# Routing attention and a gated MLP on one core: two of the four score-mask products of a pair of heads are issued in other periods

## The chip, the cores and the metric

The kernel runs on one core of one Trainium2 chip. The metric is the device time of the program in microseconds (us), the median of several runs. Beside it there is one profiled execution, from which all durations of single instructions come. The engines are TensorE (PE; PEld is its weight load), VectorE (DVE), ScalarE (ACT), GpSimd (POOL) and SyncE (SP, which issues DMAs).

## The reference

Four batches of eight heads, 768 tokens, head dimension 64, 16 centroids for each head. Each query and each key goes to the centroid that it is most similar to; a query attends to the keys of the same centroid alone. A gated MLP follows, on 3072 tokens.

```python
def _attn_ref(q, k, v, centroids):
    ...
    q_assign = np.argmax(np.einsum('bhsd,hcd->bhsc', q_n, c_n), axis=-1)
    k_assign = np.argmax(np.einsum('bhsd,hcd->bhsc', k_n, c_n), axis=-1)
    mask = q_assign[:, :, :, None] == k_assign[:, :, None, :]
    scores = scale * np.matmul(q, k.transpose(0, 1, 3, 2))
    scores = np.where(mask, scores, -1000000000.0)
    scores = scores - np.max(scores, axis=-1, keepdims=True)
    attn = np.exp(scores)
    attn = attn / (np.sum(attn, axis=-1, keepdims=True) + 1e-09)
    return np.matmul(attn, v).astype(np.float32)

def _moe_ref(x, w_in, w_out):
    h = x @ w_in
    sp = np.maximum(h, 0.0) + np.log1p(np.exp(-np.abs(h)))
    return ((h * erf(sp)) @ w_out).astype(np.float32)
```

## The kernel before

**Pairs, halves, periods.** The 32 heads are worked on as 16 pairs (p = 0 to 15). A pair's two heads lie in partitions 0 to 63 (e = 0) and 64 to 127 (e = 1), so a matrix product over the 64 numbers of one head uses one half of the TensorE array's rows. Each pair has 12 units: two halves of 384 queries times six blocks of 128 keys. Two units make a period, so that a pair has six periods, i = 0 to 5 (`period(p, i)`, line 720). Periods 0 to 2 work on the first half of the queries, 3 to 5 on the second.

**Order.** Each engine takes its instructions in the order in which the program issues them (`InOrder`, line 55). So the order in which `period` calls things is the order on each engine. In a period TensorE gets:

1. in periods 0 and 3 `turn` (line 390): six small products that turn the row maxima into rows; ScalarE then writes them as two casts into the row "shift" of the mask tile `qm`;
2. `step_ahead(u)` (line 711), one step of the row maxima, mostly of the next pair: two products `wide<-kv,qv` and two `wide<-km,qm`, and after them a reduction on VectorE (`nmx<-wide`);
3. place 0 for a mask product;
4. `products` (line 410) of the two units: queries times keys, into two score banks `sc`, in fp32;
5. place 1 for a mask product;
6. `step_ahead(u + 1)`, as in 2;
7. `scores` (line 423) of the two units: four products `sc<-qm,km` in bf16 that add the mask and the shift to the score banks;
8. place 2 for a mask product;
9. in period 3 `similarities` of the pair after the next;
10. `attend` (line 453) of the two units of the period before: eight products `turned<-pr,in_v`, over all 128 rows;
11. in periods 0 and 3 the sums of the curves for the division (`turned<-more_out,minus`).

ScalarE gets, between these, `curve` of each of the two units (exp of the score bank, `pr<-sc`), and small jobs of the weights, which are brought into another number form during attention: in period 1 `size_and_rest`, in period 2 `sign` (line 245, tile `x_own` or `x_more`), in period 3 `size_and_rest`, in period 4 `sign` of a second piece, for as long as there are early pieces (22 of them, so `sign` of period 2 runs in pairs 1 to 11). Periods 4 and 5 also have a copy of the keys and of the queries into bf16 (`kv`, `qv`), and periods 0 and 3 the two casts of `turn`.

**Mask products.** The masks of the next pair come from `hotT`, which holds a one at each token's centroid: queries in partitions 0 to 63, keys in partitions 64 to 127. `masks(p, nm, half, bank)` (line 350) issues one bf16 product with `pick` as weights, over the 64 rows of queries or of keys, for one half of the tokens, and gives back the copy that is to follow on ScalarE: Relu into `qm` for queries, Identity with a bias tile and a scale into `km` for keys. Each pair needs four of them: ("q", 0), ("q", 1), ("k", 0), ("k", 1). The keys' two halves and the first half of the queries are read from period 3 on by `step_ahead`, the second half of the queries from period 0 of the next pair on.

`MASKS` (line 51) says in which period and place each is issued; pair 0 has a table of its own, `FIRST_MASKS`. A product goes into the bank `turned[0]` in periods 0 and 5 and into `turned[1]` in the others. These two banks also hold the value products (`turned[half]`) and the other small results, at other times. In places 0 and 1 the copy is issued at once after the product; in place 2 it is issued on ScalarE between the two curves:

```python
        mask(0)()
        ...
        mask(1)()
        if u > 0:
            step_ahead(u + 1)
        ...
        scores(u)
        scores(u + 1)
        later = mask(2)
        ...
        curve(u)
        later()
        curve(u + 1)
```

After attention the MLP runs from line 891 on, with products over all 128 rows.

Of the kernel before, what the change touches and what calls it, by code (L numbers as in the profile page):

```python
# [47 lines left out]
NPT = NJ + 2  # L48
N_LATE = 10
LAST_X = 11  # L50
MASKS = {(0, 1): ("k", 0), (0, 2): ("k", 1), (2, 0): ("q", 0), (5, 0): ("q", 1)}
FIRST_MASKS = {(2, 0): ("k", 0), (2, 1): ("q", 0), (2, 2): ("k", 1), (5, 0): ("q", 1)}


# [17 lines left out]
def kernel(  # L72
# [647 lines left out]
    def period(p, i):  # L720
# [4 lines left out]
        def mask(place):  # L725
            which = (MASKS if p else FIRST_MASKS).get((i, place))
            if which:
                return masks(p + 1, *which, turned[0 if i in (0, 5) else 1])
            return lambda: None
# [261 lines left out]
```

## Time and profile before

| | us |
|---|---|
| median of 3 runs | 1022.72 (1022.52 to 1022.75) |
| profiled execution | 1022.77 |
| its span, first to last instruction | 1021.1 |
| first and last value product of attention (`turned<-pr,in_v`), start | 24.7 and 435.9 |
| one pair (period 2 of pair 5 to period 2 of pair 6, first `sc`) | 26.39 (158.51 to 184.90) |
| a mask product, `turned<-hotT,pick`, 64 rows, 384 columns, median | 0.32 |
| copy of a key mask (`km<-turned,nbig`), mean | 0.58 |
| copy of a query mask (`qm<-turned`, 128 partitions), mean | 0.49 |
| one of the two casts of `turn` (`qm<-turned`, 1 partition), mean | 0.47 |
| a curve (`pr<-sc`), mean | 0.81 |
| mean granted clock of TensorE | 1.000 |

The profile's lines all name line 63, the helper that records each operation, so that instructions are told apart by their tiles: "out<-in". A matmul's duration is longer than what it holds the array for, since successive ones are pipelined; the start-to-start time tells what one costs. In the timeline, equal instructions that follow each other are merged into one line, with their number at its end. Tiles named `more_out` among the inputs of `sc` are transposed queries and keys of every third pair, which are kept there.

### The profile page before, as it was taken

Reading aid. Unit: us, or ns where it says so; the run is one execution under the profiler, and the core shown is the slowest. Engines: PE = TensorE matmul, PEld = TensorE weight load, DVE = VectorE, ACT = ScalarE, POOL = GpSimd, SP = SyncE. Lnnn points to the kernel's source line nnn. Section 1 sums busy time; section 2 is a strip of 40 time slices with the busy share of each in tenths; the row PEclk is TensorE's granted clock in tenths of the full one; section 3 lists DMA queues with packets and bytes.
Section 4 is the critical chain, followed back from the end, with each engine's and each line's share of the span. In section 5 each row is a group of like instructions: output and inputs, shape, how many; then the busy total and the mean of one; then the engine's idle time right before and its main releaser. Section 6 shows DMA issues by size and latency. Waiting matters only on the chain.

```text
span 1021.1 us, 15464 instructions
## 1 busy us (share of the span) xinstructions
PE 1013.9 (99%) x5930; PEld 726.1 (71%) x5930; DVE 695.8 (68%) x1305; ACT 515.0 (50%) x673; POOL 345.7 (34%) x229
## 2 busy tenths in 40 slices
PE   8999999999999999999999999999999999999998
PEld 3555555554555445478888888888888888888887
DVE  8777777777777777778875674756565547565754
ACT  3787877787777666567615142322233141505050
POOL 1777777777777667745130000000000000000000
PEclk9999999999999999999999999999999999999999
DMA  9344444444343311041100100110011000000001
GB/s 214 68 98 97 104 104 103 104 104 104 83 104 87 76 28 32 24 154 61 42 1 21 63 1 1 42 42 1 1 41 42 1 21 22 1 1 21 21 1 41
DMA packets 141641, 55.55 MB, mean 54 GB/s; under 512 B 127104, under 2 KB 131456, under 8 KB 141568
## 3 DMA queue, kind: packets, MB, share of 16 engines
q1 hardware_dynamic: 139216, 54.28, 20.8%
q8 instruction: 46, 0.75, 0.3%
q10 hardware_dynamic: 2352, 0.30, 0.2%
q14 instruction: 27, 0.22, 0.1%
HBM read 41.98 MB, written 12.58 MB: 53 GB/s over the span
## 4 chain that ended last, share of the span: by engine, by line
PE 97%; DVE 1%; POOL 0%; ACT 0%; issue 0%; DVEq 0%; ACTq 0%; POOLq 0%
PE bank L63 43%; PE turned L63 33%; PE sc L63 15%; PE wide L63 7%; DVE nmx L63 1%; POOL more_out L63 0%; DVE sims L63 0%; ACT inv L63 0%; DVE kT L63 0%; DVE qT L63 0%; ACT pr L63 0%; DVE hotT L63 0%; DVE wide L63 0%; DVE den L63 0%; DVE hot L63 0%
## 5 line engine op out<-in xcount | busy, mean ns | idle before, releaser
L63 POOL TENSOR_TENSOR more_out<-more_out,pr 128x768 f32<-128x768 f32 x128 | 223.5, 1746 | 67.6 <-ACT pr L63 62.5
L63 DVE TENSOR_REDUCE nmx<-wide 128x2 f32<-128x768 f32 x189 | 180.7, 956 | 95.1 <-PE wide L63 70.8
L63 ACT ACTIVATE pr<-sc 128x768 f32<-128x768 f32 x192 | 147.0, 810 | 75.0 <-PE sc L63 75.0
L63 PE MATMUL turned<-pr,in_v 128*64 128x386 f32 x768 | 145.5, 500 | 0.1
L63 DVE TENSOR_TENSOR g<-bank,g 128x256 f32<-128x256 f32 x222 | 89.5, 421 | 52.9 <-PE bank L63 46.3
L63 PE MATMUL bank<-x_own,w_in 128*128 128x256 f32 x424 | 104.5, 380 | 0.0
L63 PE MATMUL bank<-w_out,g 128*128 128x256 f32 x448 | 103.1, 379 | 0.0
L63 PE MATMUL sc<-qT,kT 64*128 64x384 f32 x528 | 99.7, 484 | 0.0
L63 PEld LDWEIGHTS turned<-pr,in_v 128*64 128x64 f32 x768 | 46.7, 136 | 72.2 <-issue 71.1
L63 PEld LDWEIGHTS bank<-w_out,g 128*128 128x128 f32 x448 | 85.2, 190 | 11.5
L63 PEld LDWEIGHTS bank<-x_own,w_in 128*128 128x128 f32 x424 | 80.4, 190 | 12.1 <-issue 1.2
L63 ACT COPY g<-bank 128x256 f32<-128x256 f32 x28 | 10.4, 372 | 152.5 <-PE bank L63 148.5
L63 DVE TENSOR_TENSOR osb<-bank,osb 128x256 f32<-128x256 f32 x87 | 35.4, 420 | 72.8 <-ACT osb L63 25.4
L63 ACT ACT_TABLE_LOAD x48 | 61.6, 1283 | 45.7 <-DVE g L63 45.0
L63 POOL TENSOR_TENSOR more_out<-pr,pr 128x768 f32<-128x768 f32 x32 | 58.8, 1837 | 58.5 <-ACT pr L63 58.5
L63 PE MATMUL bank<-x_more,more_in 128*128 128x256 f32 x296 | 76.0, 379 | 0.0
L63 PEld LDWEIGHTS <-qv 64*128 64x128 bf16 x384 | 25.6, 93 | 65.2 <-issue 51.1
L63 PE MATMUL wide<-kv,qv 64*128 64x384 bf16 x378 | 69.4, 328 | 1.1 <-ACT km L63 0.6
L63 PEld LDWEIGHTS sc<-qT,kT 64*128 64x128 f32 x528 | 56.6, 187 | 16.6 <-issue 1.2
L63 PE MATMUL wide<-km,qm 64*128 64x384 bf16 x378 | 68.3, 322 | 0.0
L63 PE MATMUL bank<-more_out,g_more 128*128 128x256 f32 x272 | 64.3, 379 | 0.0
L63 DVE TENSOR_TENSOR g<-a_s,g 128x512 f32<-128x512 f32 x96 | 62.4, 688 | 1.4 <-ACT a_s L63 1.4
(162 smaller groups left out, 1710.2 us busy)
## 6 DMA issues: line engine op xcount, KB each, us to landing
x_own<-in_moe_w_in_dram SPq DMA_DIRECT2D x13, 512.0 KB, 4.3
in_v<-in_v_dram SPq DMA_DIRECT2D x32, 192.0 KB, 2.9
x_dram<-more_out SPq DMA_DIRECT2D x32, 192.0 KB, 2.4
x_own<-x_dram SPq DMA_DIRECT2D x6, 1024.0 KB, 5.1
out_dram<-osb SPq DMA_DIRECT2D x23, 256.0 KB, 2.0
in_k<-in_k_dram SPq DMA_DIRECT2D x59, 96.0 KB, 2.7
in_q<-in_q_dram SPq DMA_DIRECT2D x58, 96.0 KB, 3.6
g_more<-in_moe_w_out_dram SPq DMA_DIRECT2D x6, 512.0 KB, 3.6
```

The lines of the kernel that those rows point to most:

```text
L63: ins = getattr(self.engine, name)(*args, **kw)
```

## The change

One table is changed. Period and place are the key, operand and half of the tokens the value.

```diff
-MASKS = {(0, 1): ("k", 0), (0, 2): ("k", 1), (2, 0): ("q", 0), (5, 0): ("q", 1)}
+MASKS = {(0, 1): ("k", 0), (0, 2): ("q", 0), (2, 1): ("k", 1), (2, 2): ("q", 1)}
```

Before, both key products are issued in period 0 (after the `sc` products and after the scores), the first query product in period 2 ahead of the `sc` products, and the second in period 5 ahead of the `sc` products. After, period 0 has the first key and the first query product, period 2 the second key product (after the `sc` products) and the second query product (after the scores), and period 5 has none. With the products their copies move on ScalarE. In period 2, the key copy stands ahead of both curves and the query copy between them. The bank of the second query product changes from `turned[0]` to `turned[1]`. The order of the instructions on VectorE, GpSimd and SP is the same as before, and no DMA is added or moved.

## The prediction

> **What bounds the kernel now.** I read the page first: busy shares and the chain of waits.
>
> ```profile
> PE 1013.9 (99%) x5930; PEld 726.1 (71%) x5930; DVE 695.8 (68%) x1305; ACT 515.0 (50%) x673; POOL 345.7 (34%) x229
> ...
> PE 97%; DVE 1%; POOL 0%; ACT 0%; issue 0%; DVEq 0%; ACTq 0%; POOLq 0%
> ```
>
> TensorE sets the end, and all other engines have room on average. So a change is worth what it does to the time between two TensorE instructions that use the whole array. The mean granted clock is 1.000, so no clock enters the sum. The next view is the timeline of one middle pair, p = 5. I call P the start of a period's first key-query product (sc) and A the start of its first value product (turned<-pr,in_v). Period 0, TensorE (columns: start, length of the merged run, what):
>
> ```profile
> 149.71 1.45 PE L63 MATMUL sc<-more_out 64*128 64x384 f32 x8
> ...
> 151.02 0.32 PE L63 MATMUL turned<-hotT,pick 64*128 64x384 bf16 x1
> ...
> 151.36 0.63 PE L63 MATMUL sc<-qm,km 64*128 64x384 bf16 x4
> 152.01 0.32 PE L63 MATMUL turned<-hotT,pick 64*128 64x384 bf16 x1
> 152.26 1.52 PE L63 MATMUL turned<-pr,in_v 128*64 128x386 f32 x8
> ```
>
> P to A is 2.55 us here, with two mask products. Period 4, which has none, and period 5, which has one ahead of sc:
>
> ```profile
> 168.14 1.45 PE L63 MATMUL sc<-more_out 64*128 64x384 f32 x8
> ...
> 170.17 1.52 PE L63 MATMUL turned<-pr,in_v 128*64 128x386 f32 x8
> ...
> 171.96 1.61 PE L63 MATMUL sc<-more_out 64*128 64x384 f32 x8
> ...
> 174.15 1.52 PE L63 MATMUL turned<-pr,in_v 128*64 128x386 f32 x8
> ```
>
> That is 2.03 and 2.19: a lone product costs 0.16, not its 0.32 of length. It uses 64 of the 128 rows, the other half goes on, and the two halves meet again at A. Two products in one period cost 2.55 - 2.03 = 0.52, so 0.20 more than twice 0.16. ScalarE says why (period 0, then periods 2 and 3):
>
> ```profile
> 151.38 0.58 ACT L63 ACTIVATE km<-turned,nbig 128x384 bf16<-128x384 f32 x1 [0.41 <-PE turned L63]
> ...
> 151.92 0.81 ACT L63 ACTIVATE pr<-sc 128x768 f32<-128x768 f32 x1
> ...
> 152.63 0.58 ACT L63 ACTIVATE km<-turned,nbig 128x384 bf16<-128x384 f32 x1
> ...
> 153.09 0.81 ACT L63 ACTIVATE pr<-sc 128x768 f32<-128x768 f32 x1
> ```
>
> The first copy out of the bank ends at 151.38 + 0.58 = 151.96; the second product, into the same bank, starts at 152.01, and A follows 0.25 later. The copy is the wait.
>
> ```profile
> 160.71 1.52 ACT L63 ACTIVATE pr<-sc 128x768 f32<-128x768 f32 x2 [0.97 <-PE sc L63]
> 162.11 1.37 ACT L63 ACTIVATE x_more<-x_more 128x512 int16<-128x512 f32 x1
> 163.50 0.97 ACT L63 CAST qm<-turned 1x384 bf16<-1x384 f32 x2
> ```
>
> ```profile
> 158.51 1.61 PE L63 MATMUL sc<-more_out 64*128 64x384 f32 x8
> ...
> 160.70 1.52 PE L63 MATMUL turned<-pr,in_v 128*64 128x386 f32 x8
> ...
> 164.10 0.33 PE L63 MATMUL wide<-km,qm 64*128 64x384 bf16 x2
> 164.27 0.73 PE L63 MATMUL sc<-qm,km 64*128 64x384 bf16 x4
> ```
>
> Here is a second place where ScalarE holds TensorE. Both curves of period 2, the weight step sign (1.37) and the two casts of the shift run back to back. The casts end at 163.50 + 0.97 = 164.47. In single records the first score of the upper half in period 3 starts at 164.51, where 0.16 after its mask product (164.11) would have been 164.27: 0.24 lost. Pairs 1 to 11 have this wait, 0.24 to 0.25 each; in pairs 12 to 14 sign is not issued and the score comes 0.16 after, with no wait.
>
> **The change, part by part.** FIRST_MASKS stays, so pair 0 stays; pair 15 computes no next masks. 14 pairs change, p = 1 to 14. The counts of products (4), copies (4), DMAs and of all work on VectorE, GpSimd and SP stay; order changes on TensorE and ScalarE alone.
>
> *Period 5 loses its product and its copy.* It becomes period 4: 2.19 to 2.03, so -0.16 on TensorE. The 0.50 copy was in ScalarE's slack (it waits 0.20 for sc after it). VectorE follows: its next row maximum begins after the mask products, which also come 0.16 earlier. The product of the upper query half is needed in period 0 of the next pair, where it now is long done.
>
> *Period 0 changes its second product from keys to queries.* The first, the wait for its copy, and the bank stay, so the second still starts at copy end + 0.05 and A 0.25 after: 0. Its later copy is Relu with 0.48 to 0.50 in place of 0.58; what stands behind it on ScalarE, curve(u+1), comes 0.09 earlier, and Ln after that waits 0.62 for TensorE anyway.
>
> *Period 2 loses a lone product ahead of sc and gets period 0's structure.* P to A becomes 2.55 for 2.19. From single records it is 1.31 (product) + 0.36 (copy starts) + 0.58 + 0.05 + 0.25 = 2.54, so +0.35. Pair 0 shows the same composition in period 2 with the copies in the other order. ScalarE is free for the key copy: with the query copy at 159.26 gone, its last work ends at 159.37, 0.8 ahead of the new copy (P + 1.67). Behind the waiting product stand the eight value products, and then turn, the next period's mask products and sc. Bank turned[1] is free from 158.16, when VectorE's last read of it ends.
>
> *On ScalarE the query copy now stands between the two curves of period 2*, ahead of curve(u+1), sign and the casts, which TensorE already waits for. The first curve starts at P + 2.21 (period 0's row: 151.92 - 149.71) against P + 2.20 now. The query product runs from P + 2.30 to 2.62, and the curve frees ScalarE at P + 2.92, so it is the copy's turn that counts. No row has this Relu copy back to back; the like key copy takes 0.58 and the next starts 0.46 after it (152.63 to 153.09), so 0.12 overlaps; a 0.68 step before the copy at 159.26 overlaps 0.11. 0.49 - 0.11 = 0.38 is the value; the bounds are 0.36 and 0.57 (the whole key copy). The curves' steps of 0.71 and 0.69 are those between the starts 160.71, 161.42 (single records) and 162.11. Chain: 2.21 + 0.71 + 0.38 + 0.69 (second curve) + 1.39 (sign) + 0.49 + 0.47 (casts) + 0.05 = P + 6.39 for that score, against 164.51 - 158.51 = 6.00: +0.39, say +0.38 with the copy alone. TensorE's own work would allow it at P + 5.76 + 0.35 = 6.11, so the longer chain on ScalarE decides: the two delays do not add.
>
> The page "ScalarE: Activation LUTs" of the Trainium skill (What ACT_TABLE_LOAD costs) gives such an instruction with immediate operands 186 ns + 0.833 ns per element and an overlap of 93 ns: estimated 0.41 for 384 elements, which would make the end 1025.9; this case's rows are shorter by 0.03.
>
> *Sum.* Pairs 1 to 11: 0.38 - 0.16 = +0.22, times 11 = 2.42. In pairs 12 and 13 TensorE waits in period 3 for VectorE, whose first row maximum starts late:
>
> ```profile
> 346.88 0.97 DVE L63 STREAM_TRANSPOSE more_out<-in_k 128x768 f32<-128x768 f32 x1
> 347.78 0.92 DVE L63 TENSOR_REDUCE nmx<-wide 128x2 f32<-128x768 f32 x1
> ```
>
> Sc to mask products is 1.39 there (347.36 to 348.75) against 1.29 in pair 5, so 0.10 of the 0.35 is taken up: 0.35 - 0.10 - 0.16 = 0.09, twice 0.18. Pair 14: 0.35 - 0.16 = 0.19. Together 2.79. Nothing after attention takes it up: TensorE is the chain there as well. The profiled execution took 1022.77 (span 1021.1, 1.7 around it), 0.05 over the median of 1022.72: 1022.77 + 2.79 = 1025.6.
>
> **The rivals.** A, *the halves run side by side*: keys use rows 64 to 127, queries 0 to 63, and side by side a period's two products would cost 0.16 together. It decides if the query product starts when its half is done with the scores (P + 1.97) instead of after the copy (P + 2.30). A would then be at P + 2.20 in periods 0 and 2, against 2.54 in period 0's single records and 2.19: -0.34 and +0.01; with period 5's -0.16 that is -0.49 in pairs 12 to 14, and in 1 to 11, where the casts still come 0.38 later, -0.34 - 0.16 + 0.38 = -0.12: 1022.77 - 1.5 - 1.3 = 1020.0, faster. For it: 171.96, where product and sc start together. Against: both products share one bank, and 152.01 is 0.05 after the copy's end. The skill's "TensorE: Matmul & The Clock Gate" (Part 3) lets products of different row groups run at once, which is for A and agrees with 171.96; its "PSUM — Partial Sum Buffer" (PSUM bank collisions raise a hardware error) wants an engine's read of a bank guarded against another's write of it, which is against A and agrees with 152.01. By the first alone the end would be A's.
>
> B, *the copy between the curves is hidden*, if sign and the casts are not what period 3 waits for, or come no later. Then 0.24 of TensorE's 0.35 falls into the present wait: 0.35 - 0.24 - 0.16 = -0.05, 11 times -0.55, plus 0.37 from pairs 12 to 14: 1022.6, no change. For it: ScalarE is 50% busy. Against: it has no gap from 160.71 to 164.47.
>
> C, *the copy costs its full length and more*, 0.57, as the upper bound: 11 x (0.57 - 0.16) + 0.37 = 4.9, 1027.7. It needs the query product to end over 0.30 later than in period 0, for which no row speaks.
>
> **How the numbers follow.** Forecast 0.78, C 0.06, B 0.11, A 0.05. The time is the forecast's, 1025.6. About 0.2%, 2.05 us, is what a measurement of this kernel can tell from no change; the bound is 1024.8. Slower 0.84 (forecast and C), same 0.11 (B), faster 0.05 (A). The range: below, ScalarE's chain adding nothing to TensorE's 0.35, 11 x 0.19 + 0.37 = 2.5, less some uncertainty in the waits: 1024.8; above, the copy at 0.49 without overlap, 11 x 0.33 + 0.37 = 4.0, and 0.2: 1027.0.
>
> **What would show it.** P to A of 2.03 in period 5, 2.55 in periods 0 and 2; in period 2 a query product 0.05 after the key copy's end; curve, copy, curve, sign, casts without a gap on ScalarE, and the upper score of period 3 some 6.4 after P; a pair of 26.39 us (P of period 2: 158.51 to 184.90) becoming about 26.6. A query product in period 2 or 0 ahead of the copy's end, or casts no later than P + 6.0, would make it wrong.

## The result, and the profile after

The changed kernel takes 1025.23 us (median of 9 runs, 1025.15 to 1025.30) against 1022.68 in the same sets of runs for the kernel before: +2.55 us, ratio 1.0025 with a 95% interval of 1.0017 to 1.0034. It is slower, by about what was forecast (1025.6). The profiled execution took 1025.24, its span is 1023.5.

The page after, busy shares and the chain that ended last:

```profile
PE 1016.0 (99%) x5930; PEld 710.4 (69%) x5930; DVE 696.0 (68%) x1305; ACT 515.9 (50%) x673; POOL 346.2 (34%) x229
...
PE 97%; DVE 1%; POOL 0%; DMA 0%; issue 0%; ACT 0%; SPq 0%; DVEq 0%; ACTq 0%; POOLq 0%
```

TensorE is still the chain. The page alone doesn't show where 2.5 us went: neither ScalarE's 0.9 us more nor any share tells it. The timeline does. TensorE in the changed kernel, pair 5, period 0 (start, length of the merged run, what):

```profile
150.35 1.45 PE L63 MATMUL sc<-more_out 64*128 64x384 f32 x8
...
152.65 0.32 PE L63 MATMUL turned<-hotT,pick 64*128 64x384 bf16 x1
152.90 1.52 PE L63 MATMUL turned<-pr,in_v 128*64 128x386 f32 x8
```

P to A is 2.55, as before, though the second product is now one of queries. Period 5:

```profile
172.96 1.45 PE L63 MATMUL sc<-more_out 64*128 64x384 f32 x8
...
174.99 1.52 PE L63 MATMUL turned<-pr,in_v 128*64 128x386 f32 x8
```

2.03, the time of a period without a mask product; before, it was 2.19. Periods 2 and 3:

```profile
159.14 1.45 PE L63 MATMUL sc<-more_out 64*128 64x384 f32 x8
...
160.44 0.32 PE L63 MATMUL turned<-hotT,pick 64*128 64x384 bf16 x1
...
161.43 0.32 PE L63 MATMUL turned<-hotT,pick 64*128 64x384 bf16 x1
161.68 1.52 PE L63 MATMUL turned<-pr,in_v 128*64 128x386 f32 x8
...
165.08 0.33 PE L63 MATMUL wide<-km,qm 64*128 64x384 bf16 x2
165.25 0.75 PE L63 MATMUL sc<-qm,km 64*128 64x384 bf16 x4
```

P to A is 2.54 against 2.19. The second product starts 0.99 after the first, though the last of the scores between them starts at 161.09 (single records) and scores of one half follow each other 0.16 apart. The last line shows the second stall: four scores take 0.75 where an undisturbed run takes 0.49. ScalarE in the same stretch:

```profile
160.80 0.58 ACT L63 ACTIVATE km<-turned,nbig 128x384 bf16<-128x384 f32 x1 [0.79 <-PE turned L63]
161.34 0.81 ACT L63 ACTIVATE pr<-sc 128x768 f32<-128x768 f32 x1
162.05 0.48 ACT L63 ACTIVATE qm<-turned 128x384 bf16<-128x384 f32 x1
162.42 0.82 ACT L63 ACTIVATE pr<-sc 128x768 f32<-128x768 f32 x1
163.11 1.36 ACT L63 ACTIVATE x_more<-x_more 128x512 int16<-128x512 f32 x1
164.50 0.97 ACT L63 CAST qm<-turned 1x384 bf16<-1x384 f32 x2
```

The key copy ends at 160.80 + 0.58 = 161.38, and the second product on TensorE starts 0.05 later. From 160.80 on ScalarE has no gap above 0.03 until the casts end at 165.47; in single records the upper half's score starts at 165.51, P + 6.37.

Followed through all pairs by P and A, the changed kernel starts pair 1 ahead of the one before by 0.22 (start-up, which the change does not touch) and starts the last value product behind by 2.46 (438.66 against 436.20; the 435.9 in the table of the kernel before is the start of a weight load). So attention itself lost 2.68.

### The profile page after: what moved, and what is told of

It is laid out like the page before. It is cut to its first block, busy times and chain, and to the rows that moved or that the text cites. A ratio compares the mean times of both kernels' runs of the same rounds, so it can differ in the third digit from the quotient of the medians.

```text
span 1023.5 us, 15478 instructions
## 1 busy us (share of the span) xinstructions
PE 1016.0 (99%) x5930; PEld 710.4 (69%) x5930; DVE 696.0 (68%) x1305; ACT 515.9 (50%) x673; POOL 346.2 (34%) x229
## 4 chain that ended last, share of the span: by engine, by line
PE 97%; DVE 1%; POOL 0%; DMA 0%; issue 0%; ACT 0%; SPq 0%; DVEq 0%; ACTq 0%; POOLq 0%
PE bank L63 43%; PE turned L63 32%; PE sc L63 15%; PE wide L63 7%; DVE nmx L63 1%; POOL more_out L63 0%; DMA in_k<-in_k_dram 0%; SPq L63 0%; DVE kT L63 0%; DVE sims L63 0%; ACT inv L63 0%; DVE qT L63 0%; ACT pr L63 0%; DVE hotT L63 0%; DVE wide L63 0%
## 5 line engine op out<-in xcount | busy, mean ns | idle before, releaser
L63 PE MATMUL sc<-qT,kT 64*128 64x384 f32 x528 | 96.9, 484 | 0.0
L63 PE MATMUL wide<-kv,qv 64*128 64x384 bf16 x378 | 67.3, 328 | 1.1 <-ACT km L63 0.6
L63 PE MATMUL wide<-km,qm 64*128 64x384 bf16 x378 | 66.2, 322 | 0.0
L63 PEld LDWEIGHTS sc<-qT,kT 64*128 64x128 f32 x528 | 49.0, 187 | 22.6 <-issue 1.2
```

The source lines that it names most:

```text
L63: ins = getattr(self.engine, name)(*args, **kw)
```

## The experiments

Six more kernels were run, in two sets, each set beside the kernel before: it took 1022.72 in the set of the first four and 1022.95 in that of the last two. P to A is given for pair 5.

**One part undone: the second query product back in period 5.**

```diff
-MASKS = {(0, 1): ("k", 0), (0, 2): ("q", 0), (2, 1): ("k", 1), (2, 2): ("q", 1)}
+MASKS = {(0, 1): ("k", 0), (0, 2): ("q", 0), (2, 1): ("k", 1), (5, 0): ("q", 1)}
```

> The changed kernel with one part undone: the second query product goes back to period 5, ahead of sc. Period 0 keeps key and query product, period 2 has the second key product alone, after sc. Theory (the loss is the second query product's wait for the key copy in period 2, all else is free): P to A 2.54 in period 0, 2.19 in periods 2 and 5, which is before's sum, 1022.7 us. Rival 1 (the key product's new place, ahead of the second maxima step, is what costs in period 2): period 2 stays at 2.53 and period 5 gets its 0.16 back, 14 x 0.16 over the changed kernel, 1027.4. Rival 2 (the query product in period 0 gains something against the key product, hidden in the sum): below 1021.

Measured: 1022.61 us (1022.48 to 1022.82) against 1022.72 for before, ratio 0.9999 (0.9990 to 1.0009). P to A is 2.55 in period 0 (149.45 to 152.00), 2.20 in period 2 (158.24 to 160.44) and 2.19 in period 5 (171.69 to 173.88). TensorE, period 2:

```profile
158.24 1.45 PE L63 MATMUL sc<-more_out 64*128 64x384 f32 x8
...
159.54 0.32 PE L63 MATMUL turned<-hotT,pick 64*128 64x384 bf16 x1
...
160.44 1.52 PE L63 MATMUL turned<-pr,in_v 128*64 128x386 f32 x8
```

The whole loss belongs to the second query product and its copy in period 2, and both rivals fall. Exchanging keys for queries in period 0, and a lone key product behind sc in period 2 in place of a lone query product ahead of it, are each worth nothing: the periods show 2.55 and 2.20, against 2.55 and 2.19 before.

**The products spread: the second product of period 0 moved away, none after the scores.**

```diff
-MASKS = {(0, 1): ("k", 0), (0, 2): ("k", 1), (2, 0): ("q", 0), (5, 0): ("q", 1)}
+MASKS = {(0, 1): ("k", 0), (2, 0): ("q", 0), (2, 1): ("k", 1), (5, 0): ("q", 1)}
```

> Period 0 has the first key product alone (after sc), period 2 the first query product ahead of sc and the second key product after sc, period 5 the second query product ahead of sc. Theory (a second product in a period is free if it uses the other half of the rows and the copy of the first has ended by then): in period 2 the query copy ends at P + 1.23 and the key product is due at P + 1.31, so no wait, and each half gets one product, P to A 2.19; period 0 falls from 2.54 to 2.19. 14 x -0.35 = -4.9: 1017.8 us. Rival 1 (each product costs its 0.16 whatever half it uses): period 2 at 2.35, 14 x (-0.35 + 0.16) = -2.7: 1020.0. Rival 2 (any second product into the bank waits as in period 0): period 2 at 2.5, no gain, 1022.7.

Measured: 1017.89 us (1017.85 to 1018.05), ratio 0.9953 (0.9938 to 0.9968). TensorE of this run, period 2:

```profile
156.55 0.32 PE L63 MATMUL turned<-hotT,pick 64*128 64x384 bf16 x1
156.55 1.61 PE L63 MATMUL sc<-more_out 64*128 64x384 f32 x8
157.85 0.32 PE L63 MATMUL turned<-hotT,pick 64*128 64x384 bf16 x1
...
158.75 1.52 PE L63 MATMUL turned<-pr,in_v 128*64 128x386 f32 x8
```

and its ScalarE:

```profile
157.31 0.49 ACT L63 ACTIVATE qm<-turned 128x384 bf16<-128x384 f32 x1
158.25 0.58 ACT L63 ACTIVATE km<-turned,nbig 128x384 bf16<-128x384 f32 x1 [0.45 <-PE turned L63]
```

Two products in one period and one bank, and P to A is 2.20, the price of one. The query copy ends at 157.80, and the key product starts at 157.85: the copy comes off just in time, since the product is behind sc anyway. Period 0, with one product, falls to 2.21 (148.09 to 150.30). Both rivals fall. By P and A attention gains 4.66, 14 times 0.33. So a second product is free here when it uses the other half of the rows and finds the bank read.

**The same places, but both products of period 2 over the keys' rows.**

```diff
-MASKS = {(0, 1): ("k", 0), (2, 0): ("q", 0), (2, 1): ("k", 1), (5, 0): ("q", 1)}
+MASKS = {(0, 1): ("q", 0), (2, 0): ("k", 0), (2, 1): ("k", 1), (5, 0): ("q", 1)}
```

> As the run before, with the kinds exchanged: period 0 has the first query product alone, period 2 the first key product ahead of sc and the second key product after sc, both over the rows of the keys. Theory (halves count, and no wait: the first key copy ends at P + 1.33 and the second product, behind its own half's sc, is due at P + 1.45): P to A 2.35 in period 2, 2.19 in periods 0 and 5; 14 x (-0.35 + 0.16) = -2.7: 1020.0 us. Rival (halves do not count): the same as the run before, whatever that is.

Measured: 1020.12 us (1020.07 to 1020.27), ratio 0.9975 (0.9965 to 0.9985), 2.23 more than the run before it. TensorE, period 2, and the first key copy:

```profile
157.27 0.48 PE L63 MATMUL sc<-more_out 64*128 64x384 f32 x1
157.28 0.32 PE L63 MATMUL turned<-hotT,pick 64*128 64x384 bf16 x1
...
158.73 0.32 PE L63 MATMUL turned<-hotT,pick 64*128 64x384 bf16 x1
...
159.63 1.52 PE L63 MATMUL turned<-pr,in_v 128*64 128x386 f32 x8
```

```profile
158.02 0.58 ACT L63 ACTIVATE km<-turned,nbig 128x384 bf16<-128x384 f32 x1
```

P is 157.27, so P to A is 2.36: 0.16 for each product, one after the other. The second product is not held by the copy here (that ended at 158.02 + 0.58 = 158.60, and the product starts 0.13 later, not 0.05), but by its own half, which the first put back. 14 times 0.16 is 2.24, the measured difference, so the rival falls.

**The changed kernel with sign behind the division of period 3.** The weight step keeps its work and changes its place.

```diff
         elif i == 2 and early(n1):
             bounded(n1)
-            sign(n1)
...
                 part[0] = divide(u - 1)
                 next(part[0])
+        if i == 3 and early(n1):
+            sign(n1)
```

> The changed kernel with the weight step sign of period 2 issued at the end of period 3 instead, behind the division's Ln and Exp on ScalarE. The work is the same. Theory (sign between the curves and the casts is what makes the upper score of period 3 late, by 0.27 in pairs 1 to 11): that score comes 0.16 after its mask product, 11 x -0.27 = -3.0: 1022.2 us. ScalarE has 1.1 us free at sign's new place, which delays the first curve of period 4 by some 0.3; nothing on TensorE waits for it within that. Rival 1 (TensorE's own delay alone decides, the casts are on time): 1025.2. Rival 2 (the late curve or the late sum of weights on GpSimd holds something new): above 1025.2.

Measured: 1022.27 us (1022.23 to 1022.43), ratio to before 0.9996 (0.9986 to 1.0005), so 2.96 under the changed kernel. TensorE and ScalarE of this run:

```profile
163.98 0.33 PE L63 MATMUL wide<-km,qm 64*128 64x384 bf16 x2
164.14 0.49 PE L63 MATMUL sc<-qm,km 64*128 64x384 bf16 x4
```

```profile
162.30 0.97 ACT L63 CAST qm<-turned 1x384 bf16<-1x384 f32 x2 [0.16 <-PE turned L63]
...
168.60 1.33 ACT L63 ACTIVATE x_more<-x_more 128x512 int16<-128x512 f32 x1
169.82 0.81 ACT L63 ACTIVATE pr<-sc 128x768 f32<-128x768 f32 x1
```

The casts now wait for TensorE instead of TensorE for the casts, and the four scores take 0.49 again. The first curve of period 4 follows sign without a gap, and nothing on TensorE shows it. P to A of period 2 is still 2.54 (158.04 to 160.58): this takes away the stall in period 3 alone.

**The suspected wait made longer: the key copy of period 2 twice.**

```diff
-        mask(1)()
+        copy = mask(1)
+        copy()
+        if p and i == 2:
+            copy()
```

> The changed kernel with the key copy of period 2 issued twice in a row on ScalarE (pairs 1 to 14; the second writes the same values again). TensorE's instructions are the same. Theory (the second query product waits for the copy, and so does all behind it): it starts one copy step, 0.46, later, A too, and the casts of period 3 shift by the same, 14 x 0.46 = +6.5 over the changed kernel, 1031.7 us. Rival (the second product costs by its own length and place in the order, the copy's end only happens to fall beside it): the copy is hidden, 1025.2; or its delay reaches TensorE through the casts alone, 11 x 0.46 = +5.1, 1030.3, with P to A of period 2 still 2.53.

Measured: 1033.16 us (1032.95 to 1033.35) against 1022.95 for before in the same set, ratio 1.0100 (1.0085 to 1.0115). That is 10.21 over before, where the changed kernel was 2.55 over it in its own set: 7.66 more, and 6.5 was expected. ScalarE and TensorE:

```profile
163.17 1.20 ACT L63 ACTIVATE km<-turned,nbig 128x384 bf16<-128x384 f32 x2 [0.79 <-PE turned L63]
```

```profile
164.42 0.32 PE L63 MATMUL turned<-hotT,pick 64*128 64x384 bf16 x1 [0.63 <-ACT km L63]
164.67 1.52 PE L63 MATMUL turned<-pr,in_v 128*64 128x386 f32 x8
```

The product goes with the end of the copies (163.17 + 1.20 = 164.37, then 0.05), and TensorE shows it openly as idle time that the copy ended. Both rivals fall, for P to A of period 2 is 3.15 and not 2.53. The size was off because the second copy starts 0.61 after the first (163.78 in single records), not 0.46. The trace names a wait for it: the second copy waits for the semaphore that ScalarE's own instructions raise, which no other copy of that period does, and starts 0.03 after the end of the first. Both write the same part of `km`. Two key copies in a row at the start of the same run, out of two banks and into different halves of `km`, have no such wait and start 0.48 apart, 1.05 for both:

```profile
11.52 1.05 ACT L63 ACTIVATE km<-turned,nbig 128x384 bf16<-128x384 f32 x2 [3.03 <-PE turned L63]
```

P to A grows by that 0.61. In pairs 1 to 11 the score of period 3 is then less late than in the changed kernel (0.20 against 0.27), which leaves 0.53 for each by P: 11 x 0.53 + 3 x 0.61 = 7.7, the measured difference.

**The two gains together.** The table of the spread products, and sign behind the division as shown above.

> The two gains together: the table of the run spread (first key product alone in period 0, first query and second key product in period 2, second query product in period 5) and sign at the end of period 3. Theory: the 0.24 that period 3 still loses to the casts in pairs 1 to 11 is independent of the products and goes, 11 x -0.24 = -2.6 from 1017.9: 1015.2 us. Rival (with the products spread, something else on ScalarE, VectorE or GpSimd is last and takes part of it back): between 1015.2 and 1017.9.

Measured: 1015.59 us (1015.28 to 1015.63) against 1022.95 for before in the same set (1022.53 to 1023.37), ratio 0.9927 (0.9911 to 0.9944). It is the fastest of all, 7.4 us under the kernel before. TensorE, periods 2 and 3:

```profile
155.88 1.61 PE L63 MATMUL sc<-more_out 64*128 64x384 f32 x8
157.17 0.32 PE L63 MATMUL turned<-hotT,pick 64*128 64x384 bf16 x1
...
158.07 1.52 PE L63 MATMUL turned<-pr,in_v 128*64 128x386 f32 x8
...
161.64 0.49 PE L63 MATMUL sc<-qm,km 64*128 64x384 bf16 x4
```

P to A 2.19, and scores of 0.49. Against the spread products alone, the 0.24 of pairs 1 to 11 is gone (2.67 from pair 1 to pair 12, by P). The profiled run came 0.3 later out of the start-up than the spread one, and before in this set is 0.23 slower than in the other, which is why the time is 1015.6 and not 1015.2. The rival falls: nothing takes part of the gain back.

## Why the prediction was right

*Period 5.* Predicted -0.16, measured 2.19 to 2.03, -0.16. Nothing took the place of the product and its copy, and VectorE followed.

*Period 0.* Predicted 0, measured 2.55 and 2.55. The undone part shows it once more: with the change in period 0 kept, the time is that of before.

*Period 2.* Predicted +0.35 (its five terms, as printed, add up to 2.55 and not 2.54), measured 2.54 against 2.19. The cause, the wait for the key copy, is shown from both sides: the wait made longer moves the product and A with it (3.15), and a second product with no wait and in the other half costs nothing (2.20). In the trace, the second product's record waits for one semaphore, the one that ScalarE raises, and it starts 0.05 after the copy's end in the kernel before, the changed one and the one with the copy twice. No run put it into another bank. Pair 0, which the prediction took for a row of the same kind, has a third product ahead of sc; the row shows the 0.05 all the same (28.20 + 0.49, then 28.74).

*ScalarE's chain into period 3.* Predicted P + 6.39 for the upper score, measured P + 6.37 (6.00 before). The one step without a row, the query copy between the curves, was put at 0.38; it is 162.42 - 162.05 = 0.37. "ScalarE: Activation LUTs" of the Trainium skill (What ACT_TABLE_LOAD costs) gives an estimate of 0.41; the rows measure 0.37, and they decide. That the two delays do not add is shown too: the stall of period 3 grew from 0.24 to 0.27 only, while period 2 grew by 0.35. With sign out of the way the whole 0.27 goes in pairs 1 to 11, which is 2.99 by P and A and 2.96 in the medians.

*The sum.* The terms were 2.42 for pairs 1 to 11 and 0.37 for 12 to 14, together 2.79. By P and A they are 2.36 and 0.32, together 2.68: 0.21 instead of 0.22 in each of the eleven, and in pairs 12 and 13 0.07 for 0.09, as VectorE's late maximum took up 0.11. The rest of the difference to the median's +2.55 is no larger than what the start-up of a single execution varies by (0.22 between the two profiled ones). The 0.09 that is left of the distance between 1025.6 and 1025.23 is the base: the prediction added to 1022.77, and before took 1022.68 beside the changed kernel.

*The rivals.* A, the halves side by side, is a true property of the array that the changed kernel could not use, since both products go through one bank. The skill's "TensorE: Matmul & The Clock Gate" (Part 3) states it; the two runs with spread products show it with 2.20 for different halves and 2.36 for the same half. What forbade it was the bank's reader, the copy. B, the copy hidden between the curves, falls: the casts came 0.37 later, as a chain without a gap must. C, a copy at its full length, falls with the 0.37; the run with the copy twice shows where such a full length does occur, when the second copy waits for the first.

## What to carry to other kernels

In this kernel a small matrix product on the engine that sets the end was not priced by its length but by what it made the next full-array product wait for: its half of the rows, and above all the reader of the bank that it writes into. Before two of them are put into one stretch, look when the first one's copy ends; place the second where the order makes it late anyway, and in the other half. And when a copy moves to another place on its engine, count what stands behind it there up to the next thing that the bounding engine waits for: here the casts, behind a curve and a weight step.

## What the hardware did that was not expected

Two ScalarE copies of 0.58 in a row that write the same elements start 0.61 apart, where a copy into another half of `km` starts 0.48 after the one before it and a curve 0.46 to 0.55. That the semaphore is the whole reason is not shown: the two casts of `turn`, 0.47 each, have no such wait, and start 0.48 to 0.50 apart without overlapping.

And the weight loads' busy time fell from 726.1 to 710.4 us while the kernel became slower. The 5930 loads themselves are as long as before: their lengths add up to 930.9 and 930.2 us. Busy time counts moments in which at least one load runs, and what changed is how the loads of the two halves lie. A lone product ahead of sc puts one half back: in period 2 before, the loads of sc start 0.16 apart, in the changed kernel two start together every 0.32. The other runs fit: 723 to 726 us with a lone product ahead of sc in periods 2 and 5, 717 with one in period 5 alone, 710 to 711 with none. So neither this share nor TensorE's 99% tells of a change like this.
